# Six matmuls' weights moved to another byte offset, with their own transfer, and one GpSimd scaling issued earlier

## The chip, the cores and the metric

The kernel runs on one core of one Trainium2 chip. The metric is the device time of one execution in microseconds, lower is better. The core has TensorE (PE; its weight loads are listed apart as PEld), VectorE (DVE), ScalarE (ACT), GpSimd (POOL) and SyncE (SP), which issues most of the transfers.

## The reference

Three layers follow each other, all in float32: a retention attention, a mixture of 8 experts with top-1 routing, and a squared-ReLU feed-forward layer.

```python
scores = scale * np.matmul(q, k.transpose(0, 1, 3, 2))        # q, k, v: (8, 8, 576, 64)
Dmat = np.where(rel >= 0, gamma[:, None, None] ** rel[None, :, :], 0.0)
attn = np.matmul(scores * Dmat[None, :, :, :], v)
x = np.ascontiguousarray(attn.transpose(0, 2, 1, 3)).reshape(B * S, H * D)   # (4608, 512)
...
logits = x @ w_gate + modality_bias[modality_id]
e_idx = np.argmax(logits, axis=1)
...
for e in range(E):                                             # 8 experts, 512 -> 1024 -> 512
    mask = e_idx == e
    h = np.maximum(x[mask] @ w1[e], 0.0)
    out[mask] = gate_w[mask, None] * (h @ w2[e])
...
h = np.maximum(x @ w_in, 0.0)                                  # 512 -> 2048
return (h * h @ w_out).astype(np.float32)                      # 2048 -> 512
```

## The kernel before, in words

The kernel has three phases. Every float32 product of phases two and three is made of three matmuls: each operand is split into a high and a low part, and `high*high`, `high*low` and `low*high` are added in one bank. In the trace these are lines 839, 840 and 841 in phase two, and lines 1210, 1211 and 1212 in phase three. The first two of the three use the same weights.

**Phase one** (function `phase0`) goes over 36 tiles of 128 tokens. For tile t, `qk` makes the masked scores `at` and has GpSimd scale the values by their decay into `vh` (line 524). `om` multiplies `at` by `vh` on TensorE (line 558), and `xm` brings the result back to token order (line 601). The order is written out by hand: `qk(t + 1)` stands ahead of `om(t)`, so the scaling for tile t + 1 is issued one tile ahead. `vh` has three buffers. In the iteration of t = 33 the kernel also settles which expert comes first: VectorE writes the number of the table row into `eslot` (line 299), and `gather("E")` has GpSimd load it into a register, copy the row of token numbers (`ix`, line 473) and issue four indirect transfers that fetch 4 x 128 tokens into `xg` (line 476). The scaling for the last tile, t = 35, is issued in the next iteration, so it stands behind the gather on GpSimd's queue. After the loop `xg` is transposed on TensorE (line 792), split into `xh` (ScalarE, line 794) and `xl` (VectorE, line 795), and phase two begins.

**Phase two** (`phase12`) runs the experts in blocks of 512 tokens (the last three blocks have 448, 384 and 256).

**Phase three** (`phase3`) is the feed-forward layer, as a seven-product scheme over 2 x 2 blocks (products named x = 1 to 7). Weights are combinations made beforehand and kept in HBM as `wc`. The 8 slices of the hidden width are run in three passes, `PASSES = ((0, 1, 2), (3, 4), (5, 6, 7))`; in each pass the kernel goes over nine tiles of 512 tokens. Within a pass, slice q has the first-layer weights `w0q0` (high) and `w0q1` (low), and the second-layer weights `w1q0` and `w1q1`. A function `one(n, q, x)` adds six matmuls (the two contraction halves, three matmuls each) of product x for slice q, and `two(n, x)` those of the second layer. A first-layer tile holds seven combinations of 256 columns (1,024 bytes a partition), combination 6 being that of x = 3. Its slot in the pool starts at a multiple of 128 bytes, as that of every x tile does; the combinations start 16 elements, 64 bytes, into it:

```python
wt = pool_.tile([P, 7 * 256 + 32], F32R, tag="w", name=f"w{m}{j}{x}")
held["w", m, j, x] = wt[:, 16:16 + 7 * 256].rearrange("p (m c) -> p m c", m=7)
```

The second-layer weights and the x tiles start at byte 0 of their slots. The hidden values, which are the stationary operand of the second layer, start at another offset again, chosen by `[:, 56:56 + 2 * 7 * 256]`. As the program is built, every stationary operand of phase three lies 64 bytes (modulo 256) past the place of the operand that streams against it, and every stationary operand of phase two lies at the same place as the one that streams against it (0 bytes, modulo 256).

A planner (`Plan.emit`) orders the work of phase three from costs and due times; its instructions keep the order that it finds, engine by engine. In pass one x is read from `yd`, and its combinations are made on ScalarE and VectorE (`put`, line 1188 on VectorE) and stored as `xc`; in passes two and three they come back from `xc` by transfers. At the turn of a pass `loadw` issues the next weights into the same tiles, one transfer of 896 KB for each first-layer tile.

Of the kernel before, what the change touches and what calls it, by code (L numbers as in the profile page):

```python
# [9 lines left out]
F32 = mybir.dt.float32  # L10
F32R = mybir.dt.float32r
# [81 lines left out]
def kernel(ctx, tc, qT, kT, kN, vN, modT, w_gate, mbias, w1, w2, w_in, w_out,  # L93
# [54 lines left out]
    def bc(ap, shape):  # L148
        return ap.to_broadcast(shape)
# [105 lines left out]
    def tab_out():  # L255
        dve.tensor_scalar(out=tab, in0=tps, scalar1=IDOFF, scalar2=None, op0=ALU.add)
# [223 lines left out]
    def phase0():  # L480
        with ExitStack() as c0:
# [33 lines left out]

            AT, VH, XT = {}, {}, {}

            def qk(t, adv):
                b_, a, vn, kn = U[t // 4]
                x = t % 4  # L520
                cs = slice(x * P, x * P + P)
                at = wk.tile([P, H, P], F32, tag="at", name="at")
                vh = wk.tile([P, H, D], F32, tag="vh", name="vh")
                pool.tensor_tensor(out=vh, in0=vn[:, x, :].rearrange("p (h d) -> p h d", h=H),
                                   in1=bc(vdec[:, t % 9, :].unsqueeze(2), [P, H, D]), op=ALU.mult)
                mk = mask[:, 1 if t % 9 == 4 else 0, :]
                ps = [psY.tile([P, KD, P], F32, tag=f"y{i}", name=f"psa{i}") for i in range(2)]
                for c in range(KD):
                    for i in range(2):
                        r0 = 64 * i  # L530
                        pe.matmul(ps[i][:, c, :], b_[r0:r0 + 64, c, cs], a[r0:r0 + 64, c, cs],
                                  start=True, stop=True, skip_group_check=True)
                for i in range(2):
                    dve.tensor_tensor(out=at[:, KD * i:KD * i + KD, :], in0=ps[i],
                                      in1=bc(mk.unsqueeze(1), [P, KD, P]), op=ALU.mult)
                    adv(3)
                AT[t], VH[t] = at, vh

            scur = [0]

# [128 lines left out]
            for t in range(NTILE + 1):  # L669
                if t == xl_ + 1:  # L670
                    xm(xl_)
                    adv(99)
                    for _ in route_a(NG - 2):
                        pass
                if t % 4 == 1 and 2 + t // 4 < 9:
                    u = 2 + t // 4
                    alloc(u)
                    load(u, 4 * u, 4)
                if t == 4:
                    work.append(prep())  # L680
                if t + 1 < NTILE:
                    qk(t + 1, adv)
                if t < NTILE:
                    om(t)
                    if t == xl_ + 2:
                        route_c(NG - 2)
                        tab_out()
                        for _ in early():
                            pass
                        gather("E")  # L690
                        expert("E")
                        wload(("E", 0), 0)
                        wload(("E", 0), 1)
                    if t == NTILE - 1:
                        wsplit(("E", 0), 0, dve)
                        wsplit(("E", 0), 1, dve)
                        wload(("E", 1), 0)
                        wload(("E", 1), 1)
                    adv(3)
                    if t == xl_ + 1:  # L700
                        for _ in route_b(NG - 2, dve):
                            pass
                    kv(t)
                for it, fn in list(stage.items()):
                    if it == t:
                        fn()
                if t >= 1 and t - 1 != xl_:
                    xm(t - 1)
                    g, j = (t - 1) // G, (t - 1) % G
                    if j == G - 1 and g < NG - 2:  # L710
                        work.append(wrap(route_a(g)))
                        stage[t + 2] = lambda g=g: work.append(wrap(route_b(g, dve)))
                        stage[t + 4] = lambda g=g: (adv(99), route_c(g))
# [354 lines left out]
    def wload2(m, j, pool_, load=True):  # L1068
        for x in range(2):
            if m:  # L1070
                held["w", m, j, x] = pool_.tile([P, 4, 2, 256], F32R, tag="w", name=f"w{m}{j}{x}")
                if load:
                    for a in range(2):
                        n = 4 - x
                        sp.dma_start(held["w", m, j, x][:, 0:n, a, :].bitcast(F32),
                                     wc[m, PASSES[0][j], a][:, x * 1024:x * 1024 + 256 * n]
                                     .rearrange("p (m c) -> p m c", c=256))
                continue
            wt = pool_.tile([P, 7 * 256 + 32], F32R, tag="w", name=f"w{m}{j}{x}")
            held["w", m, j, x] = wt[:, 16:16 + 7 * 256].rearrange("p (m c) -> p m c", m=7)  # L1080
            if load:
                sp.dma_start(held["w", m, j, x].bitcast(F32).rearrange("p m c -> p (m c)"), wc[m, PASSES[0][j], x])

    MX = {1: 0, 2: 1, 3: 2, 5: 3, 6: 4, 7: 5, 4: 6}
    MW = {1: 0, 4: 1, 2: 2, 5: 3, 6: 4, 7: 5, 3: 6}
# [71 lines left out]
    def phase3():  # L1157
        with ExitStack() as c2:
# [41 lines left out]
            def dma(o, i, kb, r, w, early=False):  # L1200
                plan.add(m_(kb), lambda e: (pool if early else e).dma_start(o, i), r, w, 2.0)
# [15 lines left out]
            def loadw(p, m, j0=0):  # L1217
                for j, fp in list(enumerate(PASSES[p]))[j0:]:
                    for x in range(2):
                        if m:  # L1220
                            n = 4 - x
                            for a in range(2):
                                dma(WT[m][j][x][:, 0:n, a, :].bitcast(F32),
                                    wc[m, fp, a][:, x * 1024:x * 1024 + 256 * n].rearrange("p (m c) -> p m c", c=256),
                                    131 * n, [], [("w", m, j, x, a)])
                            continue
                        dma(WT[m][j][x].bitcast(F32).rearrange("p m c -> p (m c)"), wc[m, fp, x], 917,
                            [], [("w", m, j, x)])

            def xprep(n):  # L1230
                p, t = T3[n]
# [37 lines left out]
            def one(n, q, x):  # L1269
                p, t = T3[n]  # L1270
                if x == 1:
# [5 lines left out]
                z, h = ZT[u % 3], HT[u % 3]  # L1277
                kz_ = lambda *i: [("z", u % 3, j) for j in i]
                ps, kp = (X_, kx) if x in (1, 6, 7, 4) else ((Z_, kz) if x == 2 else (Y_, ky))
                w, m, mx = WT[0][q], MW[x], MX[x]  # L1280
                plan.add(MMS, six([ps, ps], [((w[0][:, m, P * k:P * k + P], w[1][:, m, P * k:P * k + P]),
                                              (XT[mx][:, 0, k, :], XT[mx][:, 1, k, :])) for k in range(2)],
                                  x in (1, 2, 5)),
                         [("w", 0, q, 0), ("w", 0, q, 1), ("x", mx, 0), ("x", mx, 1)], [kp])
                last = q == len(PASSES[p]) - 1
                if x == 1:
                    copy(z[:, 1, :], X_, 256, [kx], kz_(1))
# [161 lines left out]
```

## Time and profile before

| | |
|---|---|
| median of 3 runs | 1331.18 us |
| lowest and highest of them | 1328.75 and 1335.86 us |
| the profiled execution's own time | 1336.03 us |
| its span, first to last instruction | 1334.2 us |
| busy in that span: PE, PEld | 1294.7 us (97%), 1209.6 us (91%) |
| DVE, ACT, POOL | 1021.8 us (77%), 624.4 us (47%), 125.3 us (9%) |
| mean granted TensorE clock | 0.995 |

TensorE is busy for nearly the whole span, so the time is what its matmuls take at the pace at which they follow each other, and the waits between them. A matmul's record is longer than the distance to the next one, so that the busy share alone does not show the pace: it is read from how many matmuls start in a stretch. The profiled execution is the slowest of the four times shown.

### The profile page before, as it was taken

The page shows a single profiled execution, that of the slowest core. Times are in us where ns is not written, and L with a number is a line of the kernel's source. Part 1 is how long each engine was busy: PE and PEld are TensorE (multiplying, and loading weights), DVE is VectorE, ACT ScalarE, POOL GpSimd, SP SyncE. Part 2 cuts the span into 40 slices and gives each one's busy share as a digit, 9 for nine tenths or more (in the row PEclk, how much of TensorE's full clock was granted, in tenths as well). Part 3 has the DMA queues.
Part 4 walks back from the last instruction along what each step waited for, and adds up shares of the span by engine and source line. Part 5 has one row for each costly group of instructions (what it writes and reads, how often), then busy time and mean ns, then how long its engine had stood idle before and what let it go on. Part 6 is the DMA issues. An engine that isn't in the chain of part 4 may idle for free.

```text
span 1334.2 us, 26978 instructions
## 1 busy us (share of the span) xinstructions
PE 1294.7 (97%) x10639; PEld 1209.6 (91%) x10639; DVE 1021.8 (77%) x2095; ACT 624.4 (47%) x1283; POOL 125.3 (9%) x170
## 2 busy tenths in 40 slices
PE   7999989999999999899999999999999999999997
PEld 6888877888888888899999999999999999999997
DVE  3877858878887887666888888858788777776765
ACT  2344444545445445455656566534334344443333
POOL 3222112101110110000000000000000011111121
PEclk9999999999999999899999999999999999999999
DMA  9998257787787877789555544778799766655551
GB/s 330 391 347 304 77 197 240 265 299 275 259 297 246 304 266 250 265 289 319 228 225 217 201 174 176 283 257 308 273 344 346 270 217 216 214 193 174 174 187 51
DMA packets 152499, 331.89 MB, mean 249 GB/s; under 512 B 15440, under 2 KB 67440, under 8 KB 152368
## 3 DMA queue, kind: packets, MB, share of 16 engines
q1 hardware_dynamic: 144752, 309.82, 65.5%
q0 software_dynamic: 5840, 19.14, 4.0%
q8 instruction: 85, 1.39, 0.4%
q10 hardware_dynamic: 1776, 1.17, 0.3%
q14 instruction: 46, 0.38, 0.1%
HBM read 222.33 MB, written 107.78 MB: 247 GB/s over the span
## 4 chain that ended last, share of the span: by engine, by line
PE 43%; DVE 10%; DMA 1%; issue 1%; POOL 0%; POOLq 0%; DVEq 0%
PE bank L1211 14%; PE bank L1210 14%; PE bank L1212 14%; DVE z L1188 4%; DVE h L1320 3%; DVE z L1196 1%; DVE x L1188 1%; DVE yr L1188 1%; DMA w<-wc 1%; DMA x<-xc 1%; PE bank L839 0%; PE bank L840 0%; PE bank L841 0%; POOL out L1327 0%; DVE oe L1188 0%
## 5 line engine op out<-in xcount | busy, mean ns | idle before, releaser
L1211 PE MATMUL bank<-x,w 128*128 128x256 f32 x1008 | 282.5, 280 | 4.2 <-DVE x L1188 4.2
L1210 PE MATMUL bank<-w,h 128*128 128x256 f32 x1008 | 282.1, 280 | 2.2 <-DVE oe L1188 1.6
L1210 PE MATMUL bank<-x,w 128*128 128x256 f32 x1008 | 281.9, 280 | 2.3 <-DMA x<-xc 2.3
L1212 PE MATMUL bank<-w,h 128*128 128x256 f32 x1008 | 282.1, 280 | 0.7 <-DVE h L1320 0.7
L1212 PE MATMUL bank<-x,w 128*128 128x256 f32 x1008 | 281.8, 280 | 0.9 <-DMA w<-wc 0.9
L1211 PE MATMUL bank<-w,h 128*128 128x256 f32 x1008 | 281.6, 279 | 0.0
L1185 ACT ACTIVATE z<-bank 128x256 f32<-128x256 f32 x288 | 108.6, 379 | 255.1 <-PE bank L1212 254.3
L1211 PEld LDWEIGHTS bank<-x,w 128*128 128x128 f32 x1008 | 189.3, 188 | 5.8 <-DVE x L1188 5.8
L1212 PEld LDWEIGHTS bank<-w,h 128*128 128x128 f32 x1008 | 191.9, 190 | 1.2 <-DVE h L1320 1.1
L1212 PEld LDWEIGHTS bank<-x,w 128*128 128x128 f32 x1008 | 191.9, 190 | 1.1 <-DMA w<-wc 1.1
L1210 PEld LDWEIGHTS bank<-w,h 128*128 128x128 f32 x1008 | 189.4, 188 | 2.9 <-DVE oe L1188 2.0
L1210 PEld LDWEIGHTS bank<-x,w 128*128 128x128 f32 x1008 | 189.4, 188 | 2.6 <-DMA x<-xc 2.5
L1319 ACT ACTIVATE h<-z 128x512 fp32r<-128x512 f32 (+2 forms) x270 | 158.2, 598 | 70.7 <-DVE z L1188 55.5
L1211 PEld LDWEIGHTS bank<-w,h 128*128 128x128 f32 x1008 | 189.3, 188 | 0.0
L1320 DVE TENSOR_TENSOR h<-z,h 128x512 fp32r<-128x512 f32 (+2 forms) x270 | 168.7, 647 | 7.5 <-ACT h L1319 7.5
L1188 DVE TENSOR_TENSOR z<-z,bank 128x256 f32<-128x256 f32 x216 | 89.1, 415 | 56.6 <-PE bank L1212 41.9
L839 PE MATMUL bank<-xh,wx 128*128 128x512 f32 (+3 forms) x320 | 119.5, 373 | 4.2 <-ACT xh L794 2.8
L839 PE MATMUL bank<-hh,wy 128*128 128x512 f32 (+3 forms) x320 | 122.7, 384 | 0.0
L840 PE MATMUL bank<-xl,wx 128*128 128x512 f32 (+3 forms) x320 | 119.3, 373 | 1.0 <-DVE xl L795 1.0
L840 PE MATMUL bank<-hl,wy 128*128 128x512 f32 (+3 forms) x320 | 119.9, 375 | 0.2 <-DVE hl L856 0.2
L841 PE MATMUL bank<-hh,wy 128*128 128x512 f32 (+3 forms) x320 | 119.7, 374 | 0.0
L841 PE MATMUL bank<-xh,wx 128*128 128x512 f32 (+3 forms) x320 | 119.2, 372 | 0.0
(185 smaller groups left out, 2127.0 us busy)
## 6 DMA issues: line engine op xcount, KB each, us to landing
x<-xc SPq DMA_DIRECT2D x112, 512.0 KB, 5.6
wr<-w SPq DMA_DIRECT2D x80, 512.0 KB, 4.4
xc<-x SPq DMA_DIRECT2D x63, 512.0 KB, 3.7
wc<-cwh SPq DMA_DIRECT2D x16, 896.0 KB, 5.8
wc<-cwl SPq DMA_DIRECT2D x16, 896.0 KB, 6.5
w<-wc SPq DMA_DIRECT2D x16, 896.0 KB, 7.8
pd<-oe SPq DMA_DIRECT2D x24, 512.0 KB, 3.9
xd<-xs SPq DMA_DIRECT2D x9, 1024.0 KB, 5.4
```

The source lines that it names most:

```text
L839: pe.matmul(ps, lh, rh, start=first, stop=False)
L840: pe.matmul(ps, lh, rl, start=False, stop=False)
L841: pe.matmul(ps, ll, rh, start=False, stop=last)
L1185: plan.add(a_(c), lambda e: e.activation(o, i, f), r, w)
L1188: plan.add(engs or d_(c), lambda e: e.tensor_tensor(out=o, in0=a, in1=b, op=op), r, w)
L1196: e.scalar_tensor_tensor(out=z, in0=z, scalar=0.0, in1=z, op0=ALU.max, op1=ALU.mult)
L1210: e.matmul(ps[n], lh, rh, start=first and n == 0, stop=False, skip_group_check=True)
L1211: e.matmul(ps[n], lh, rl, start=False, stop=False, skip_group_check=True)
L1212: e.matmul(ps[n], ll, rh, start=False, stop=True, skip_group_check=True)
L1319: plan.add(a_(c), lambda e: e.activation(h[:, 0, a:b], z[:, a + 1:b + 1], AF.Copy), rs, ks[0])
L1320: plan.add(d_(c), lambda e: e.tensor_tensor(out=h[:, 1, a:b], in0=z[:, a + 1:b + 1], in1=h[:, 0, a:b].bitcast(F32), op=ALU.subtract), rs + ...
```

## The change: what it does

**In phase three** the first-layer tiles of the first slice of every pass (q = 0) are laid out anew. Their combinations 0 to 5 stay where they were, 64 bytes into the slot. Combination 6 starts at element 64 + 6 x 256, so that it lies at byte 0 of a 256-byte line of the slot, at the same place (modulo 256) as the x that streams against it. It is read by the six matmuls `one(n, 0, 3)`, once for each of the 27 pairs of pass and tile. Since the tile is no longer one piece, its load becomes two transfers, of 768 and of 128 KB, and the planner is given two keys for them: the six combinations and the seventh are waited for, and waited on, apart. The other tiles (q = 1, 2) keep one transfer.

**In phase one** the scaling of the last tile's values is issued in the iteration of t = 33, behind the table's conversion and ahead of `early()` and `gather("E")`. `qk(35)` then finds it done.

```diff
+            def vscale(t):
+                vh = VH[t] = wk.tile([P, H, D], F32, tag="vh", name="vh")
+                pool.tensor_tensor(out=vh, in0=U[t // 4][2][:, t % 4, :].rearrange("p (h d) -> p h d", h=H),
+                                   in1=bc(vdec[:, t % 9, :].unsqueeze(2), [P, H, D]), op=ALU.mult)
+
             def qk(t, adv):
...
-                vh = wk.tile([P, H, D], F32, tag="vh", name="vh")
-                pool.tensor_tensor(out=vh, in0=vn[:, x, :].rearrange("p (h d) -> p h d", h=H),
-                                   in1=bc(vdec[:, t % 9, :].unsqueeze(2), [P, H, D]), op=ALU.mult)
+                if t not in VH:
+                    vscale(t)
...
                         route_c(NG - 2)
                         tab_out()
+                        vscale(t + 2)
                         for _ in early():
                             pass
                         gather("E")
...
-            wt = pool_.tile([P, 7 * 256 + 32], F32R, tag="w", name=f"w{m}{j}{x}")
-            held["w", m, j, x] = wt[:, 16:16 + 7 * 256].rearrange("p (m c) -> p m c", m=7)
+            held["w", m, j, x] = pool_.tile([P, 7 * 256 + 64], F32R, tag="w", name=f"w{m}{j}{x}")
             if load:
-                sp.dma_start(held["w", m, j, x].bitcast(F32).rearrange("p m c -> p (m c)"), wc[m, PASSES[0][j], x])
+                for a, b in spans(j):
+                    sp.dma_start(w0at(m, j, x, a, b).bitcast(F32), wc[m, PASSES[0][j], x][:, 256 * a:256 * b])
+
+    def spans(j):
+        return ((0, 7),) if j else ((0, 6), (6, 7))
+
+    def w0at(m, j, x, a, b):
+        o = 16 if j or a < 6 else 64
+        return held["w", m, j, x][:, o + 256 * a:o + 256 * b]
...
-                        dma(WT[m][j][x].bitcast(F32).rearrange("p m c -> p (m c)"), wc[m, fp, x], 917,
-                            [], [("w", m, j, x)])
+                        for a, b in spans(j):
+                            dma(w0at(m, j, x, a, b).bitcast(F32), wc[m, fp, x][:, 256 * a:256 * b], 131 * (b - a),
+                                [], [("w", m, j, x, a)])
...
-                w, m, mx = WT[0][q], MW[x], MX[x]
-                plan.add(MMS, six([ps, ps], [((w[0][:, m, P * k:P * k + P], w[1][:, m, P * k:P * k + P]),
+                m, mx = MW[x], MX[x]
+                w = [w0at(0, q, a, m, m + 1) for a in range(2)]
+                a = 6 if m == 6 and not q else 0
+                plan.add(MMS, six([ps, ps], [((w[0][:, P * k:P * k + P], w[1][:, P * k:P * k + P]),
...
-                         [("w", 0, q, 0), ("w", 0, q, 1), ("x", mx, 0), ("x", mx, 1)], [kp])
+                         [("w", 0, q, 0, a), ("w", 0, q, 1, a), ("x", mx, 0), ("x", mx, 1)], [kp])
```

On GpSimd, around the gather for the first expert, the kernel before has 29 scalings, then the register load of `eslot`, the copy of the token numbers, the four transfers, and the last scaling:

```order
L524 TENSOR_TENSOR vh<-v,vdec 128x512 x29
L471 TENSOR_LOAD eslot
L471 ISA x2
L473 ISA
L473 COPY ix<-tab 128x4
L476 DMA xg<-xd,ix 128x512 x4
L524 TENSOR_TENSOR vh<-v,vdec 128x512
```

In the changed kernel the same place reads:

```order
L520 TENSOR_TENSOR vh<-v,vdec 128x512 x30
L471 TENSOR_LOAD eslot
L471 ISA x2
L473 ISA
L473 COPY ix<-tab 128x4
L476 DMA xg<-xd,ix 128x512 x4
```

The last scaling has moved ahead of the register load, into the row of the others; nothing else moved on this engine.

On SP's queue, at the turn from pass one to pass two, the kernel before issues the last store of partial results (`pd`), then the four first-layer tiles and the reload of `pd` into `yr` (the number behind a name is that of the buffer):

```order
L1201 DMA pd_97<-oe_10378 128x1024 x2
L1201 DMA w000_10159<-wc_96 128x1792
L1201 DMA w001_10161<-wc_96 128x1792
L1201 DMA w010_10163<-wc_96 128x1792
L1201 DMA w011_10165<-wc_96 128x1792
L1201 DMA yr_10376<-pd_97 128x1024 x2
L1201 DMA w101_10317<-wc_96 128x3x256 x2
```

The changed kernel has here:

```order
L1213 DMA w000_10159<-wc_96 128x1536
L1213 DMA pd_97<-oe_10380 128x1024
L1213 DMA w001_10162<-wc_96 128x1536
L1213 DMA pd_97<-oe_10380 128x1024
L1213 DMA w000_10159<-wc_96 128x256
L1213 DMA w001_10162<-wc_96 128x256
L1213 DMA yr_10378<-pd_97 128x1024
L1213 DMA w010_10165<-wc_96 128x1792
L1213 DMA w011_10167<-wc_96 128x1792
L1213 DMA yr_10378<-pd_97 128x1024
L1213 DMA w101_10319<-wc_96 128x3x256 x2
```

The larger pieces of the two split tiles have moved ahead of the stores, and two small transfers stand behind them. On VectorE and ScalarE nothing moved but a few neighbours; on TensorE only some groups of six changed places with a neighbour at the two turns of a pass.

## Rows read from the trace of the kernel before

**Rows 1.** The page: one of the six groups of phase-three matmuls.

```profile
L1210 PE MATMUL bank<-x,w 128*128 128x256 f32 x1008 | 281.9, 280 | 2.3 <-DMA x<-xc 2.3
```

**Rows 2.** Timeline, 159 to 180 us: start us, us, engine, line, operation.

```profile
166.00 0.19 POOL L473 COPY ix<-tab 128x4 int32 x1 [13.97 <-DVE eslot L299]
...
166.36 1.09 PE L558 MATMUL bank<-at,vh 128*64 128x128 f32 x16
167.02 1.16 POOL L476 DMA_INDIRECT xg<-xd,ix  x1 [0.84 <-POOL ix L473]
...
167.85 1.19 PE L601 MATMUL bank<-iwg,xt 128*128 128x136 f32 x8
...
168.97 0.67 PE L552 MATMUL bank<-q,sbs 64*64 64x128 f32 x16
...
170.99 0.95 POOL L476 DMA_INDIRECT xg<-xd,ix  x1 [0.30 <-issue]
...
171.96 1.05 POOL L524 TENSOR_TENSOR vh<-v,vdec 128x512 f32<-128x512 f32 x1
...
173.06 1.34 PE L558 MATMUL bank<-at,vh 128*64 128x128 f32 x16 [3.42 <-POOL vh L524]
...
174.34 3.50 PE L601 MATMUL bank<-iwg,xt 128*128 128x136 f32 x16
...
177.68 1.91 PE L792 MATMUL bank<-ident,xg 128*128 128x128 f32 x16
...
178.44 2.07 ACT L794 ACTIVATE xh<-bank 128x512 fp32r<-128x512 f32 x4
```

**Rows 3.** DMA issues of 170.95 to 172 us: median us to landing.

```profile
xg<-xd,ix POOLq DMA_INDIRECT x1, 4.7
```

**Rows 4.** Busy us and granted clock (PEclk) in two stretches of five us.

```profile
core 0: us, PE busy (x) PEld busy (x) DVE busy (x) ACT busy (x) POOL busy (x), PEclk, DMA share, GB/s
170.00:175.00 5.00, 1.94 (x19) 1.61 (x20) 0.98 (x3) 1.68 (x2) 2.68 (x3) 0.88 0.91 327
175.00:180.00 5.00, 5.00 (x33) 4.69 (x33) 3.07 (x4) 3.40 (x12) 0.00 (x0) 0.78 0.46 154
```

**Rows 5.** Phase three between waits: stretch, its length, PE busy, matmuls, granted clock.

```profile
609.30:632.30 23.00, 23.00 (x197) 1.00 0.98 304
634.90:663.00 28.10, 28.10 (x251) 1.00 0.63 240
...
840.00:882.00 42.00, 42.00 (x373) 1.00 0.73 268
...
888.40:1026.90 138.50, 138.50 (x1178) 1.00 0.86 309
...
1030.00:1044.40 14.40, 14.40 (x124) 1.00 0.75 262
...
1053.90:1318.00 264.10, 264.10 (x2245) 1.00 0.54 190
...
1323.40:1326.00 2.60, 2.60 (x26) 1.00 0.00 0
```

**Rows 6.** The end of phase two: busy us, matmuls in brackets, granted clock.

```profile
595.00:605.00 10.00, 10.00 (x85) 10.00 (x85) 2.92 (x5) 2.48 (x5) 0.00 (x0) 1.00 0.99 392
```

**Rows 7.** Weight loads at 595:605, 640:660 and 895:995 (two): busy us, mean ns.

```profile
L841 PEld LDWEIGHTS bank<-hh,wy 128*128 128x128 f32 x16 | 3.1, 192 | 0.0
...
L1212 PEld LDWEIGHTS bank<-x,w 128*128 128x128 f32 x37 | 6.9, 188 | 0.0
...
L1212 PEld LDWEIGHTS bank<-x,w 128*128 128x128 f32 x144 | 27.7, 192 | 0.0
L1210 PEld LDWEIGHTS bank<-x,w 128*128 128x128 f32 x144 | 27.0, 188 | 0.0
```

**Rows 8.** Waits of TensorE in phase three: us in total, times, longest.

```profile
PE bank L1211 <- DVE x L1188: 4.2, 8, 1.1
PE bank L1210 <- DMA x<-xc: 2.3, 1, 2.3
```

More of the change, by code (lines that the diff above doesn't have):

```diff
@@ L536, in qk @@
                     adv(3)
-                AT[t], VH[t] = at, vh
+                AT[t] = at
             scur = [0]
```

## The prediction

> **What bounds the kernel now.** I read the page first: TensorE is busy for 97% of the span, and the six groups of phase-three matmuls (1,008 each, so 6,048 in all) carry the largest shares [rows 1]. What they cost is set by how closely they follow each other and by the waits between them. The list of TensorE's waits gives little for phase three: 4.2 us in eight waits for VectorE's x, one of 2.3 us for a transfer [rows 8]. So I looked at the pace, in stretches of phase three that no wait breaks [rows 5]. A record is 0.28 us long, so that about 2.5 of those counted in a stretch began ahead of it. 634.9 to 663 us then gives 28.1 / (251 - 2.5) = 0.1131 us for one matmul, 840 to 882 gives 0.1134; but 609.3 to 632.3 gives 0.1182, 888.4 to 1026.9 gives 0.1178, 1030 to 1044.4 gives 0.1184, and 1053.9 to 1318 again 0.1178. They are the same instructions on the same tiles, at a granted clock of 1.00 throughout. There are two paces, 113.3 and 117.8 ns, and TensorE stays in the one it has until it waits. After the eight waits of pass one (the first stretch shown begins at 634.9, the last at 840) it goes on at the fast pace, and so it does at 1323.4; from 888.4, 1030.0 and 1053.9 it is slow. At the end of phase two, where weights and streamed operand lie at the same place modulo 256 bytes, 256-column matmuls follow each other at 10.0 / (85 - 2.4) = 0.121 us [rows 6], a third pace.
>
> The weight loads show the difference from inside [rows 7]: at the end of phase two all of them take 192 ns; in a fast stretch all take 188; in a slow stretch line 1212 takes 192 and line 1210 takes 188. The slow pace is thus a cycle of three, with one held-up load in it, whichever weights are read.
>
> Phase one has one long wait: the last tile's `at` x `vh` matmuls sit 3.42 us for GpSimd's scaling, which runs at 171.96 only after the four gather transfers (167.02 to 171.94) have been issued [rows 2].
>
> **The change part by part.** *The scaling.* GpSimd idles 13.97 us ahead of the token-number copy at 166.00 [rows 2], and the scaling takes 1.05 us; it goes into that idle time and cannot delay the gather. The wait from 169.64 (168.97 + 0.67) to 173.06 ends. The last tile's 16 matmuls would then take 1.09 us as the tile before did, and the two returns to token order twice 1.19, so that TensorE could be at the transposes at 169.64 + 1.09 + 2.38 = 173.1 instead of 177.68. But there the gathered rows are late next: the fourth transfer, issued at 170.99, lands 4.7 us later [rows 3], at 175.7, and the first chunk needs all four. `xh` then begins near 176.0 instead of 178.44: 2.4 us. Above, the gain is 4.4 us, if the data itself can be used sooner than the record of its landing says; below it is 1.0, if the fourth weight load of the expert, which is set free by the earlier split and so runs sooner, shares the transfer engines with the gather. I take 2.4, the row's value. The granted clock was 0.88 and 0.78 in the ten microseconds behind the wait [rows 4]; TensorE still idles some 3 us for the gather, so I credit nothing for it. Everything behind (router, table, expert E) hangs on this chain and moves up with it.
>
> *The six matmuls.* 162 matmuls (27 times six) get the placement of phase two. If they take its pace, they cost 162 x (121 - 113.3) = 1.2 us against the fast pace, 0.5 us against the slow one.
>
> *The pace around them.* This is the large term. Four slow stretches add up to 23.0 + 138.5 + 14.4 + 264.1 = 440 us [rows 5]. At the fast pace they are 440 x (1 - 113.3 / 117.8) = 16.8 us shorter. The new group comes once a tile, and by the program's order 60 to 130 matmuls stand ahead of the first one in a pass or behind a wait, some 250 in all at 4.5 ns, which leaves 15.7 us. Whether the group does this is not shown by any row: it breaks the cycle of three, as a wait does, and the nearest rows for a break are the waits, of which nine (eight in pass one, and 1323.4) were followed by the fast pace and three by the slow one. That is why I take the fast pace as the likelier outcome. The other end of this term is a loss, below.
>
> *What is late next.* At the fast pace pass one already waits 4.2 / 8 = 0.5 us a tile for VectorE [rows 8]. The 17 further tiles of passes two and three could come to wait as much, 9 us in all; but there x is loaded and not made, and the list has a single wait of 2.3 us for such a transfer. I take 2 us, between 0 and 9.
>
> *The split loads.* Each turn of a pass has two more transfers on SP's queue, and the larger pieces leave ahead of the `pd` stores. What waits there is the 2.3 us for x and what hides under it; I take 0, between -1.5 and +1.5, since both sides are a shift of one or two issues.
>
> The profiled execution's own time is 1336.0 us, 4.8 above the median of the runs shown, whose spread of 7 us is what one stretch like 888 to 1027 (5.3 us between the paces) or 1054 to 1318 (10.1 us) makes by falling one way or the other. The sum is 1336.0 - 2.4 + 1.2 - 15.7 + 2.0 = **1321.1 us**.
>
> **A rule that speaks against the change.** The Trainium skill, "TensorE: Matmul & The Clock Gate", in "Step-by-step: what each phase is for", has TensorE read its streamed operand and its weights by two independent ports, so that loading the next weights takes nothing from the running matmul. Its table in "Back-to-back issue gap" gives 262 cycles, 109.2 ns at 2.4 GHz, for 256 columns. By that the place of the weights does not matter and the 6,048 matmuls would be a constant 660 us. The trace does not agree: none of its three paces is 109.2 ns, and they go with the time of a load.
>
> **The rivals.** *The group leaves TensorE in the slow pace.* For it speaks the one place where such matmuls pass into the others with no wait: phase two ends at 121 ns, and 609.3 to 632.3 runs at 118.2 [rows 5, 6]. Each tile would be slow from the group to the next wait. Pass one, fast for 247 us, would lose up to 247 x (117.8 / 113.3 - 1) = 9.8 us, less the waits for VectorE that a slower TensorE no longer meets (4.2 us, and the restart of each, some 0.1): 4.8 us net at most, nothing if the waits swallow the rest. Time: 1336.0 - 2.4 + 0.5 + (0 to 4.8) = 1334 to 1339. It ends slower than before by more than 0.5% once more than four fifths of pass one's loss is real, from 1337.8 us. Against it: this is one case, entered from another loop.
>
> *The pace does not follow the placement.* The group costs nothing and changes nothing: only the scaling is left, 1336.0 - 2.4 = 1333.6, and the stretches fall as they did in the runs shown, 1327 to 1334. It is what the rule above amounts to. The loads of 192 ns speak against it.
>
> *The group switches the pace now one way, now the other.* Half of the 440 us is won (8.4) and half of pass one's 4.8 lost: 1336.0 - 2.4 + 0.9 - 8.4 + 2.4 = 1328.5, or some us above.
>
> **How the numbers follow.** A measurement of this kernel can tell about 0.5% from no change: 1324.5 and 1337.8 us around the median of 1331.18. The fast pace gets 0.45 (0.42 below 1324.5, the rest within), its own range 1316 to 1329 from the bounds of its terms. The slow pace gets 0.33, half of it slower by over 0.5%. The untouched pace gets 0.12, all of it no change. The mixture gets 0.10, 0.02 of it faster. That makes 0.44 faster, 0.39 the same, 0.17 slower. The range has to reach to the slow pace: 1316 to 1338.
>
> **What would show it.** The scaling: GpSimd's last `vh` ends ahead of the token-number copy, line 558 waits for it no more, and the transposes wait for `xg` near 175.7; were they at 173, the landing was not the limit. The pace: windows of passes two and three count 113.3 ns a matmul and all loads take 188 ns but the six of each tile, at 192. If the stretch behind the first group, from some 617 us, still runs at 118 and pass one behind its groups as well, the first rival is right. If pass two and three at the fast pace wait for x by more than 2 us, that term was too small. The forecast is wrong in its main step if the six matmuls, though slower themselves, leave the pace of what follows as it was.

## The result and the profile after

The changed kernel takes 1339.59 us, median of five runs (1336.82 to 1340.55), against 1329.60 us (1328.59 to 1335.86) for the kernel before, measured beside it: a ratio of 1.0067, 95% interval 1.0038 to 1.0097. It is slower, by more than the 0.5% that the prediction set as the bound. The profiled execution took 1337.11 us, with a span of 1335.3 us and a granted clock of 0.994. That is only 1.1 us above the profiled execution of before, which at 1336.03 us lay above all five runs of that kernel here. So the two traces must be compared by stretches, not by their ends.

In the changed kernel lines 1222, 1223 and 1224 are what 1210, 1211 and 1212 were, 562 was 558, 605 was 601, 797 was 792, 799 was 794, 844 was 839, and 1200 was 1188.

The page of the changed kernel, the group that answers to [rows 1]:

```profile
L1222 PE MATMUL bank<-x,w 128*128 128x256 f32 x1008 | 283.0, 281 | 1.8 <-DMA x<-xc 1.8
```

Phase three of the changed kernel in stretches, to set against [rows 5] (stretch, length, PE busy with its matmuls, PEld, DVE, ACT, POOL, granted clock, DMA share, GB/s):

```profile
634.80:645.50 10.70, 10.70 (x97) 10.70 (x96) 7.41 (x15) 4.19 (x9) 0.00 (x0) 1.00 0.96 382
...
694.80:705.30 10.50, 10.50 (x95) 10.50 (x94) 7.28 (x16) 4.21 (x8) 0.00 (x0) 1.00 1.01 375
706.50:723.20 16.70, 16.70 (x144) 16.70 (x143) 16.48 (x37) 12.76 (x27) 0.00 (x0) 1.00 0.24 96
...
906.50:1009.50 103.00, 103.00 (x876) 103.00 (x875) 85.55 (x185) 43.39 (x96) 0.00 (x0) 1.00 0.85 311
1066.00:1320.00 254.00, 253.59 (x2153) 253.39 (x2151) 188.78 (x404) 113.00 (x263) 34.71 (x64) 1.00 0.53 188
```

With 2.5 of the counted matmuls begun ahead of each stretch, as in the prediction, these are 10.7 / 94.5 = 0.1132 us, 0.1135, 0.1180, 0.1179 and 253.6 / 2150.5 = 0.1179 us for one matmul. In pass one six of the nine tiles now have both paces. The first stretch begins behind a wait and is fast; 645.5 is where the six matmuls at byte 0 come, and the next wait ends the slow stretch behind them. At 694.8 it is the same, and 706.5 to 723.2 shows the slow part. Passes two and three, where few waits interrupt, are slow almost throughout, from the group at 906 and from the one at 1065 us on. Counted over the starts of all 6,048 matmuls, 850 run at the fast pace and 5,154 at the slow one, the rest beside waits; in the profile of before it was 2,193 and 3,808.

Weight loads of the changed kernel at 906.5 to 1009.5 us and at 635 to 645 us (busy us, mean ns), to set against [rows 7]:

```profile
L1222 PEld LDWEIGHTS bank<-x,w 128*128 128x128 f32 x146 | 28.0, 192 | 0.0
...
L1223 PEld LDWEIGHTS bank<-x,w 128*128 128x128 f32 x147 | 27.6, 188 | 0.0
...
L1222 PEld LDWEIGHTS bank<-x,w 128*128 128x128 f32 x12 | 2.3, 188 | 0.0
```

The slow pace is again a cycle of three with one load of 192 ns. This time it is the first of the three that is held up (line 1222), not the third; which one it is is thus not tied to a line.

TensorE's waits in phase three of the changed kernel (us in total, times, longest), to set against [rows 8]:

```profile
PE bank L1222 <- DMA x<-xc: 1.8, 1, 1.8
PE bank L1222 <- DVE oe L1200: 1.6, 2, 0.8
PE bank L1223 <- DVE x L1200: 1.5, 2, 1.0
```

The wait for VectorE's x has shrunk from 4.2 us in eight to 1.5 us in two, as a slower TensorE leaves VectorE more time.

The end of phase one in the changed kernel, to set against [rows 2] (start us, us, engine, line, operation):

```profile
166.25 0.19 POOL L473 COPY ix<-tab 128x4 int32 x1 [7.69 <-DVE eslot L299]
...
169.82 1.09 PE L562 MATMUL bank<-at,vh 128*64 128x128 f32 x16
...
171.25 0.95 POOL L476 DMA_INDIRECT xg<-xd,ix  x1 [0.30 <-issue]
...
174.56 0.33 PE L797 MATMUL bank<-ident,xg 128*128 128x128 f32 x1 [0.73 <-DMA xg<-xd,ix]
175.83 0.33 PE L797 MATMUL bank<-ident,xg 128*128 128x128 f32 x1 [0.94 <-DMA xg<-xd,ix]
176.47 0.45 PE L797 MATMUL bank<-ident,xg 128*128 128x128 f32 x1 [0.32 <-DMA xg<-xd,ix]
177.43 2.85 PE L797 MATMUL bank<-ident,xg 128*128 128x128 f32 x13 [0.51 <-DMA xg<-xd,ix]
...
180.04 0.48 PE L844 MATMUL bank<-xh,wx 128*128 128x512 f32 x1
```

The wait for `vh` is gone, and the last `at` x `vh` matmuls start at 169.82 as foreseen. But TensorE then waits for the gathered rows. The fourth transfer, issued at 171.25, takes this long to land, against 4.7 us in [rows 3] (DMA issues of 171.2 to 172.2 us):

```profile
xg<-xd,ix POOLq DMA_INDIRECT x1, 6.1
```

And in this profile the clock falls behind the waits. Columns as in the stretches above:

```profile
173.80:177.40 3.60, 1.12 (x4) 0.43 (x3) 0.00 (x0) 0.51 (x3) 0.00 (x0) 0.88 0.99 338
...
177.40:180.00 2.60, 2.57 (x12) 2.57 (x13) 1.26 (x2) 1.54 (x3) 0.00 (x0) 0.51 0.36 126
```

TensorE is busy for 1.12 of the 3.6 us ahead, and the thirteen transposes behind it then run at a granted clock of 0.51, the lower level, 1.2 GHz. From the token-number copy to the first matmul of phase two it is 180.04 - 166.25 = 13.79 us, against 179.34 - 166.00 = 13.34 in the profile of before. The scaling moved; nothing was gained.

### The profile page after: what moved, and what is told of

The parts are those of the page before. It is cut to its first block, busy times and chain, and to the rows that moved or that the text cites. A ratio compares the mean times of both kernels' runs of the same rounds, so it can differ in the third digit from the quotient of the medians.

```text
span 1335.3 us, 26992 instructions
## 1 busy us (share of the span) xinstructions
PE 1300.3 (97%) x10639; PEld 1215.2 (91%) x10639; DVE 1024.7 (77%) x2095; ACT 626.0 (47%) x1283; POOL 125.1 (9%) x170
## 3 DMA queue, kind: packets, MB, share of 16 engines
q8 instruction: 85, 1.39, 0.4%
## 4 chain that ended last, share of the span: by engine, by line
PE 51%; DVE 3%; DMA 1%; POOL 0%; issue 0%; POOLq 0%; DVEq 0%
PE bank L1223 17%; PE bank L1222 17%; PE bank L1224 17%; DVE z L1200 1%; DVE h L1335 1%; DMA x<-xc 1%; PE bank L844 0%; PE bank L845 0%; PE bank L846 0%; DVE z L1208 0%; POOL out L1342 0%; DVE oe L1200 0%; DVE x L1200 0%; DVE yr L1200 0%; POOLq L1460 0%
## 5 line engine op out<-in xcount | busy, mean ns | idle before, releaser
L844 PE MATMUL bank<-xh,wx 128*128 128x512 f32 (+3 forms) x320 | 119.5, 373 | 4.1 <-ACT xh L799 2.7
L846 PE MATMUL bank<-hh,wy 128*128 128x512 f32 (+3 forms) x320 | 119.5, 373 | 0.0
```

Of the source, the lines that this page charges most:

```text
L844: pe.matmul(ps, lh, rh, start=first, stop=False)
L846: pe.matmul(ps, ll, rh, start=False, stop=last)
```

## The experiments

Each was timed against the kernel before on its own chip: the first four on one, the next four on a second, the last four on a third. The kernel before itself had a median of 1339.8, 1328.5 and 1329.1 us there. The times in microseconds that were expected for the first four go by the first measurement, in which it had 1329.6; on their chip, ten microseconds slower, only the ratios and the profiles can be held against them.

```
                             median us   ratio to before, 95%
scaling alone                1336.19     0.9974 (0.9958 to 0.9990)
bytes alone                  1341.18     1.0013 (0.9998 to 1.0028)
transfers alone              1338.16     0.9991 (0.9975 to 1.0007)
pass one kept                1339.02     0.9989 (0.9975 to 1.0003)

whole change                 1338.98     1.0075 (1.0046 to 1.0103)
group at 128                 1324.11     0.9961 (0.9930 to 0.9992)
group at 192                 1325.69     0.9963 (0.9935 to 0.9992)
short matmuls                1339.19     1.0072 (1.0037 to 1.0107)

gather first                 1328.74     0.9998 (0.9968 to 1.0029)
whole change at 128          1325.27     0.9966 (0.9941 to 0.9991)
at 128, gather first         1322.03     0.9942 (0.9918 to 0.9965)
200 columns each tile        1326.72     0.9989 (0.9968 to 1.0011)
```

### The parts of the change, each alone

**The scaling alone** is the change without its edits to phase three.

> Only the scaling is issued earlier; phase three is as before. Theory (the loss is phase three's pace, and the scaling gives nothing because the gather lands later): line 558's wait of 3.4 us is gone, the first line-839 matmul of phase two starts between 179.3 and 180.3 us (179.34 before), pass one runs at 113.3 ns between its waits, and the time is that of before, 1328 to 1336 us. Rival (the scaling gives its 2.4 us and phase three alone hides it): phase two starts near 177 us. Rival (the earlier scaling is itself the loss): 1336 to 1340 us.

It is faster, by 3.5 us on that chip (1.3 to 5.6 by the interval). Its profile shows the chain that the prediction meant:

```profile
167.19 0.19 POOL L473 COPY ix<-tab 128x4 int32 x1 [7.70 <-DVE eslot L299]
...
172.19 0.95 POOL L476 DMA_INDIRECT xg<-xd,ix  x1 [0.31 <-issue]
175.91 0.80 PE L797 MATMUL bank<-ident,xg 128*128 128x128 f32 x3
177.02 1.64 PE L797 MATMUL bank<-ident,xg 128*128 128x128 f32 x13 [0.31 <-DMA xg<-xd,ix]
178.41 0.48 PE L844 MATMUL bank<-xh,wx 128*128 128x512 f32 x1
```

From the copy to phase two it is 11.22 us, 2.1 less than before: the theory that the scaling gives nothing by itself is refuted. Counted from the copy at 166.00 of before, phase two would start at 177.2, near the 177 of the rival. The rest of the 3.5 us lies within the interval. The last transposes can start 177.02 - 172.19 = 4.8 us after the fourth transfer's issue, and take their full speed. The 2.57 us by which the whole change is worse here (13.79 - 11.22) are the landing (177.43 - 171.25 = 6.18 against 4.83, so 1.35) and the clock (177.43 to 180.04 is 2.61 against 1.39, so 1.22).

**The bytes alone** are the change without the scaling; **the transfers alone** split the loads and keys in the same way, but leave combination 6 at 64 bytes:

```diff
-        o = 16 if j or a < 6 else 64
+        o = 16
```

> Only the new layout of the first slice's tile with its split transfers; the scaling stays where it was. Theory: every group at byte 0 leaves TensorE at 117.8 ns until a wait; all of pass one is slow from group to wait, some 850 fast matmuls are left of 6,048, and the time is 1336 to 1340 us. Rival (the scaling or the gather made the loss): 1329 to 1334 us and pass one fast.

> The split transfers, keys and order of the change without the new place: the seventh combination stays 64 bytes into the slot, the scaling where it was. Theory (the place does it): pass one fast between its waits, over 2,000 fast matmuls, 1328 to 1336 us. Rival (the split transfers and the planner's order do it): pass one slow after the group of x = 3, 1336 to 1340 us.

The transfers alone make no difference that can be measured, and their profile has 3,124 fast matmuls. The bytes alone have 1,442 (850 were expected), and every group at byte 0 is followed by the slow pace, up to the next wait. (The order of phase three's matmuls is the same in the two kernels; the count shifts by some tens with the border between the paces, so that two expectations below have 1,464 and 5,682 for what is 1,442 and 5,643 here.) Against the kernel before they are hardly slower, 1.0013, on a chip on which that kernel took ten us more than on the others. The profiles of this chip also have up to 7 us of waits for ScalarE's z, which the first two lack (3.7 us in six with the bytes alone); what makes them was not tried.

**Pass one kept** is the whole change with combination 6 at 64 bytes in pass one and at byte 0 in passes two and three.

```diff
-    def w0at(m, j, x, a, b):
-        o = 16 if j or a < 6 else 64
+    def w0at(m, j, x, a, b, p=0):
+        o = 16 if j or a < 6 or p == 0 else 64
```

> The whole change, but in pass one the seventh combination is put and read 64 bytes into the slot; byte 0 holds from pass two on. Theory: pass one is fast again (about 2,100 matmuls at 113.3 ns, eight waits for VectorE of 0.3 to 1.1 us), passes two and three are slow as in the change: some 3 to 5 us less than the change, 1332 to 1336 us. Rival (the loss lies in passes two and three, where the transfers are split too): 1337 to 1340 us.

Pass one is slow from 606 to 692 us and fast from there to 879, with pace changes only where TensorE waits: the part at 606 to 692 was not expected. From pass two on each group at byte 0 turns it slow or finds it slow (at 879, 903, 1062, 1182, 1212 and 1242 us it was fast ahead), and only waits bring the fast pace back, which in pass three they do several times. The pace follows the byte within one execution. That pass one is worth 3 to 5 us is not shown, since the whole change was not timed on this chip.

**The whole change** once more, on another chip:

> The whole change once more, on the same chip as the runs beside it. Theory (the six matmuls at byte 0 leave TensorE in the slow pace, the earlier scaling gives one to two us back): between the scaling alone (0.9974 of before) and the placement alone (1.0013), that is 0.998 to 1.001 where before itself is slow for much of passes one to three, and up to 1.007 where before is fast there. In the profile each group at byte 0 of pass one begins a slow stretch that ends at the next wait. Rival (the loss of the first measurement belonged to its chip): 0.995 or less.

The loss is there again, 1.0075, and so is the pattern in the profile: 1,071 fast matmuls, each group at byte 0 followed by a slow stretch.

### The same group at other bytes

Only the offset of combination 6 differs from the bytes alone: 128 and 192 bytes past a multiple of 256.

```diff
-        o = 16 if j or a < 6 else 64
+        o = 16 if j or a < 6 else 32
```

The second kernel has 48 there in place of 32 (elements of 4 bytes). The bytes are counted from the start of the slot. As the programs are built, all these slots and the x tiles start at the same place modulo 256, so each number is also the distance to the operand that streams against the weights.

> As the placement alone, but the six matmuls' weights begin 128 bytes past a multiple of 256 in place of 0 (the other weights 64 bytes past). If only the coincidence with the streamed operand's place (both at byte 0) sets off the slow pace, the group runs at 113 or 118 ns like its neighbours, the pace behind it is the one ahead of it, and the time is that of the split transfers alone, 0.998 to 1.001 of before. If any step in the place of the weights does it, each group begins a slow stretch and fewer than 1,500 of the 6,048 matmuls are fast, as with byte 0 (1,464). If this place instead brings TensorE into the fast pace, more than 4,500 are fast and the time is some 8 us below before.

> The same with 192 bytes past a multiple of 256. The same three outcomes: the pace carried through (about half the matmuls fast, 0.998 to 1.001), the slow pace behind each group (fewer than 1,500 fast, about 1.001), or the fast pace behind each group (more than 4,500 fast, 0.994 or less).

Both are the third outcome, the fast pace behind each group, with 5,643 and 5,580 fast matmuls. By their medians they are 4.3 and 2.8 us below before, less than the 8 us expected: half of the 35 runs of the kernel before on this chip lie between 1322.7 and 1328.5 us, well below the profiled 1336.0, so that it was likely fast for long stretches in them, which no profile shows. Pass three of the kernel with 128 bytes in one stretch, and its waits for VectorE's x:

```profile
1048.00:1303.00 255.00, 255.00 (x2248) 254.87 (x2247) 194.70 (x416) 114.55 (x270) 34.72 (x64) 1.00 0.57 201
```

```profile
PE bank L1222 <- DVE x L1199: 4.4, 8, 1.2
```

That is 255 / 2245.5 = 0.1136 us for one matmul, where the changed kernel takes 0.1179. The table counts, for each of the 27 groups of a profile, the pace ahead (the mean of 15 distances between starts) and behind (14 distances from the eighth matmul on); fast is below 114.2 ns, slow above 116.8. Where a wait falls among the 14 distances, a group can come out as mixed.

```
                        the six    fast ahead,   fast ahead,   slow ahead,   slow ahead,
place, kernel           themselves fast behind   slow behind   fast behind   slow behind
  0 whole change        119.5 ns        0             8             0            19
  0 whole change again  119.6           0            10             0            17
  0 bytes alone         119.4           0            11             0            13   (3 mixed)
 64 transfers alone     115.7          12             0             0            12   (3 mixed)
128 group at 128        117.6          27             0             0             0
128 whole change at 128 117.8          24             0             3             0
128 at 128, gather first  117.8          23             0             4             0
192 group at 192        113.5          25             0             2             0
```

At 64 bytes, where all the other weights lie, the group carries the pace through. At 128 and 192 bytes it leaves TensorE fast, also in the nine cases in which it was slow ahead, although at 128 bytes the six themselves take 117.6 ns on average (unevenly, from 113 to 123 ns by their place in the six). At byte 0 it leaves TensorE slow. Between the whole change and the group at 128 bytes on the same chip lie 14.9 us. Only the weights were moved, never x: whether their own place counts, their distance to x, or the step from the 64 bytes of their neighbours, these runs do not tell.

### A matmul of another width in the sequence

The kernel before with a narrow copy of the slice's first matmul ahead of each slice of each tile:

```diff
+                    if short:
+                        e.matmul(ps[0][:, :short], pairs[0][0][0], pairs[0][1][0][:, :short], start=True, stop=False, skip_group_check=True)
...
+                                  x in (1, 2, 5), WIDTHS[(u + u // 9) % 9] if x == 1 else 0),
```

> The kernel before with one more matmul ahead of each slice of each tile in phase three (72 in all), a narrow copy of the slice's first matmul that this one then overwrites; its width goes through 32, 64, 96, 128, 160, 192, 224, 240 and 200 columns, each eight times. It costs 72 times some 30 to 110 ns, 5 us in all. If the pace is a state of the sequence that anything irregular can switch, it changes at many of these 72 places, in a way that goes with the width and the pace ahead, and with some width the pace behind is fast nearly every time. If the pace goes with the operands and the waits alone, it changes at none of them, and the time is before plus 5 us (1.004).

It costs 10.7 us (1.0072), twice what was expected; in the profiles phase three is 3.0 us longer than before (720.3 against 717.3), and what makes the rest was not looked into. One of the narrow matmuls (line 1212), with the matmuls ahead and behind:

```profile
1197.82 0.28 PE L1215 MATMUL bank<-w,h 128*128 128x256 f32 x1
...
1198.61 0.28 PE L1216 MATMUL bank<-w,h 128*128 128x256 f32 x1
1198.72 0.22 PE L1212 MATMUL bank<-x,w 128*128 128x128 f32 x1
1198.78 0.33 PE L1214 MATMUL bank<-x,w 128*128 128x256 f32 x1
...
1199.07 0.28 PE L1216 MATMUL bank<-x,w 128*128 128x256 f32 x1
...
1199.89 0.28 PE L1214 MATMUL bank<-w,h 128*128 128x256 f32 x1
```

Seven distances take 0.79 us ahead (113 ns each) and 0.82 behind (117). No wait lies between, and the operands are those of every tile. By width, those beside a wait left out (from, to; for the very first, of 32 columns, the pace ahead is that of the end of phase two):

```
columns   fast-fast  fast-slow  slow-fast  slow-slow
   32         0          6          0          1
   64         0          2          1          5
   96         0          1          5          1
  128         0          3          4          0
  160         0          4          0          3
  192         0          0          2          3
  200         5          0          2          0
  224         3          0          0          5
  240         0          3          4          0
```

128 and 240 columns switch the pace each time, 224 keep it, 160 end in the slow one, 200 in the fast one. So the pace is a state of the sequence, which something irregular can set either way, and not a property of the weights that are being read.

**200 columns each tile** uses that: one such matmul ahead of the first slice of each tile, 27 in all, and nothing else.

> The kernel before with one matmul of 200 columns ahead of the first slice of each tile in phase three (27 in all, 90 ns each, 2.4 us). In the run with narrow matmuls of nine widths each of the eight of 200 columns was followed by the fast pace, whichever pace was ahead. Theory (the pace is a kept state of the sequence of starts): TensorE is slow only from a wait to the next such matmul, more than 4,500 of the matmuls are fast, and the time is that of the placement at 128 bytes plus 2.4 us, 0.997 to 0.999. Rival (the operands' places alone decide, and the eight were chance): half the matmuls are slow as in before, and the time is 1.002.

25 of the 27 are followed by the fast pace, and 4,949 matmuls are fast. Most of pass three in one stretch:

```profile
1105.20:1300.00 194.80, 194.80 (x1721) 194.80 (x1721) 144.79 (x307) 85.54 (x202) 30.44 (x56) 1.00 0.52 186
```

194.8 / 1718.5 = 0.1134 us. Phase three, from its first to its last matmul of 256 columns, takes 707.2 us against 717.3 in the profile of before. The median is 2.3 us below before, 0.9989, but the interval includes 1.

### The landing of the gather

The scaling alone, with the second pair of expert E's weight loads held behind a 16-byte transfer that reads the gathered rows:

```diff
+                        sp.dma_start(gs, XG["E"][0][0:1, :, 0:1].rearrange("p j d -> p (j d)"))
                         wload(("E", 1), 0)
                         wload(("E", 1), 1)
```

> The scaling alone, and the second pair of expert E's weight loads kept back on SP's queue by a 16-byte transfer that reads the gathered rows, so that they start only when the rows have landed. Theory (the rows land late because the weight loads share the transfer engines): the fourth gather transfer lands about 4.7 us or less after its issue, 11.2 us or less lie between the token-number copy and the first matmul of phase two (13.3 in the kernel before, 11.2 to 13.8 in the kernels with the early scaling so far), and the time is 2 to 4 us below before, 0.997 to 0.9985. Rival (the landing has nothing to do with the weight loads): the fourth transfer takes 6 us again. Against the edit: the second pair is needed for expert E's third and fourth slice at about 184 us; if it lands later than that, TensorE waits there and the gain is lost.

The chain does what the theory says: the fourth transfer lands 4.5 us after its issue, and 10.93 us lie between the copy and phase two. The time shows nothing (0.9998), since phase three is left as it was: this profile has 4,380 slow matmuls, and the runs spread from 1321.6 to 1337.3 us. With the pace set by 128 bytes the same edit can be seen:

> The whole change with the six matmuls' weights 128 bytes past a multiple of 256 in place of 0. With the placement alone at 128 bytes 5,682 of 6,048 matmuls were fast (0.9961). With the earlier scaling on top, if the two add, 0.994 to 0.995, more than 5,500 fast, and the time within 1,318 to 1,325 us. If the earlier scaling gives nothing in company, 0.996.

> The same and the second pair of weight loads kept back. If both theories hold it is the fastest of all, 1 to 2 us below the whole change at 128 bytes, about 0.993 of before. If the loads are missed later, it is equal or slower than that kernel.

In the whole change at 128 bytes the fourth transfer takes 6.4 us, and 13.75 us lie between copy and phase two, so the scaling is worth nothing there, and the time is the 0.996 that was expected for this case. Its weight loads go out while the rows are being gathered (start us, us):

```profile
166.27 8.00 SPq L439 DMA_DIRECT2D wr<-w  x5
```

With the gather first, two go out ahead of the gather and the others behind it:

```profile
165.59 0.97 SPq L440 DMA_DIRECT2D wr<-w  x2
165.60 0.19 POOL L474 COPY ix<-tab 128x4 int32 x1 [7.68 <-DVE eslot L300]
...
170.61 0.95 POOL L477 DMA_INDIRECT xg<-xd,ix  x1 [0.30 <-issue]
...
174.94 1.64 PE L799 MATMUL bank<-ident,xg 128*128 128x128 f32 x13 [1.47 <-DMA xg<-xd,ix]
175.06 0.77 SPq L703 DMA_DIRECT2D gs<-xg  x1
176.05 1.70 SPq L440 DMA_DIRECT2D wr<-w  x3
176.34 0.48 PE L846 MATMUL bank<-xh,wx 128*128 128x512 f32 x1
```

The rows land in 4.3 us, the held loads start at 176.05, and phase two begins 10.74 us after the copy, 3.0 less. The median is 3.2 us lower than without the edit on the same chip. This is the fastest kernel of the study, 0.9942 of before.

## Why the prediction was wrong, step by step

**The pace around the six** (-15.7 us) is the step that failed. The prediction said that the group "breaks the cycle of three, as a wait does", and took the fast pace as the likelier outcome, because nine of twelve waits were followed by it. That the group sets the pace was right: 27 groups of 27. That it sets the fast one was wrong: the slow pace follows all 27, also the eight that were fast ahead, and in place of 15.7 us less, phase three is 1.2 us longer. Which pace it sets was taken from the wrong rows. A wait and a group of matmuls at another byte are different disturbances, and the tally of waits says nothing about the second. The one place of the trace where matmuls at byte 0 pass into the others with no wait, 595:605 into 609.3:632.3 [rows 5, 6], showed the slow pace, and stood in the prediction as a rival with 0.33. The group at 128 bytes shows that the term was of the right size for another offset: phase three takes 705.2 us there (on another chip), against 718.5 in the changed kernel and 717.3 in the one before, so 12.1 us less where the terms of phase three come to 12.5 (15.7 - 1.2 - 2.0). That the fast pace was there to be had by moving these six weights was thus right; that byte 0 is the place for it was a guess, and it did not hold.

**That rival's price** was nearly right. It gave 1334 to 1339 us; the profiled execution took 1337.1, and the median, 1339.6, lies 0.6 above it and 1.6 above the whole range. Without the 2.4 us that it credits to the scaling it is 1336.5 to 1341.3. Its two sides are in the traces: 1,346 more slow matmuls (5,154 - 3,808) at 4.5 ns are 6.1 us, and what TensorE loses in the gaps of phase three (all that distances between starts of over 130 ns have above 118) fell from 14.9 to 9.8 us. Phase three came out 1.2 us longer than in the profile of before. The larger difference of the medians, 10 us, is argued and not traced, as the one profile of the kernel before took 1336 us and none near its median exists. For it speak the spreads (1322.7 to 1340.7 us over 35 runs of the kernel before on one chip; 1336.8 to 1341.8 for the 17 runs of the changed kernel), and three profiles with the very same sequence of matmuls in phase three: 2,193 matmuls are at the fast pace in before, some 1,650 in gather first, some 3,700 in scaling alone. With the place of before the same code can run fast for long; both profiles of the changed kernel are slow for most of phase three.

**The six matmuls** (+1.2) are mis-sized: they take 119.5 ns, and among slow neighbours that is 162 x (119.5 - 117.8) = 0.3 us.

**The scaling** (-2.4) is mis-sized. The wait for `vh` went as foreseen, and alone it gave 2.1 us in its profile; in the four profiles of it together with byte changes (and no gather first) it gave 0.9, 0.7, -0.4 and -0.4 (12.43, 12.67, 13.75 and 13.79 us from copy to phase two, against 13.34). Two costs ate it. The landing of 4.7 us in [rows 3] was one value of a spread: with the early scaling it was 4.8 to 6.4 in five profiles, and with the second pair of weight loads kept back 4.5 and 4.3. That mechanism was named in the prediction, but priced at 1.4 us at most. The other was credited with nothing: in three of the five the clock falls to its lower level while TensorE waits for the rows (the granted clock is 0.51, 0.65 and 0.61 from the last transposes to phase two), and that stretch takes 2.61, 2.13 and 2.30 us; in the other two it stays at 1.00, and 1.39 us are enough.

**What is late next** (+2.0) did not arise, since the fast pace did not come. Where it did come, at 128 bytes, the wait for VectorE's x stayed at 4.4 us in eight, and all the gaps of phase three came to 18.0 us, 3.1 more than in the profile of before: the estimate was fair.

**The split loads** (0) were right: 0.9991, with an interval that includes 1.

**The rule that spoke against the change.** The weights' place decides 14.9 us on one chip between kernels that otherwise differ in the early scaling only. The Trainium skill, "TensorE: Matmul & The Clock Gate", in "Step-by-step: what each phase is for", describes streamed operand and weights as read by two independent ports. The prediction took from it that the weights' place does not matter; the runs do not agree with that, though they do not show that the reading of the weights is what holds TensorE up. Its 109.2 ns and 660 us were no fit figures for this stream, which follows at 113.3 or 117.8 ns. The Trainium skill, "TensorE: Matmul & The Clock Gate", in "Back-to-back issue gap", gives that table for the gap of an isolated matmul and says that in a stream with weight loads both set the distance.

What stays open is why byte 0 ends in the slow pace and 128 bytes in the fast one. The runs show the transitions, not what lies behind them.

## What to carry to other kernels

Where the same matmuls show two paces with no wait between them, first find what sets the pace, by putting a disturbance of several kinds into one run and counting what follows each, before paying for one particular disturbance. A nearest analogue of the same kind, even a single one, weighs more than a tally of something else. And a gain on a chain that ends in a transfer needs the spread of that transfer's landing, what else uses the transfer engines at that moment, and what the clock does while TensorE waits for it.

## What the runs showed of the hardware

The pace of 256-column float32 matmuls with a weight load for each was 113.3 or 117.8 ns for the same instructions, and stayed for up to 264 us (the slow one, in the kernel before [rows 5]). It was switched without any wait by a matmul of another width, or by six matmuls whose weights lay at another byte (0: to slow, 119.5 ns themselves; 192: to fast, 113.5 ns; 128: to fast, though 117.7 ns themselves). The gathered rows of the same four transfers landed 4.3 to 6.4 us after the fourth issue, quickest with the later ones of the 512 KB weight loads kept back. And in the changed kernel 3.6 us of a TensorE that was busy for a third of them were followed by 2.6 us at a granted clock of 0.51.
